# Loading the raw blocks of background jobs one unit ahead, in a mixture-of-experts kernel on one Trainium2 core

## The chip, the cores and the metric

The kernel runs on one core of a Trainium2 chip, as one launch. The metric is the device time of a launch in microseconds (us). Three runs of the kernel before took 2087.25, 2093.49 and 2100.9 us; the median, 2093.49, is the time to beat.

## The reference

Three layers follow each other on 2304 token rows of width 512: a windowed attention with global tokens, a mixture of 8 experts whose gate is normalised over rows and columns eight times, and a two-layer network with an ELU between.

```python
x = attention(q_l, k_l, v_l, q_g, k_g, v_g)         # (2304, 512) after the reshape
P = normalised_gate(x @ w_gate)                      # (2304, 8)
out = 0
for e in range(8):
    out += P[:, e:e+1] * (np.maximum(x @ w1[e], 0) @ w2[e])   # w1[e]: 512x1024, w2[e]: 1024x512
h = out @ w_in                                       # 512 x 2048
g = np.where(h > 0, h, np.exp(np.minimum(h, 0)) - 1)
return (g @ w_out).astype(np.float32)
```

## The kernel before, in words

**Arithmetic.** Every product of matrices is taken in two parts: an operand is split into a high part (suffix h) and a low rest (suffix l), and three matmuls (`three`, line 146: hh, lh, hl) replace one. Above that stands a scheme of Strassen's kind: a 2x2 block product is made of 7 block products, numbered 1 to 7, from sums and differences of blocks. Those sums have to be built, split and kept: x sums for the tokens, `t1`..`t4` for the weights.

**Units.** A unit is one half (512 of 1024 hidden columns) of one expert, so there are 16. The tokens are cut in two parts, and each unit is passed over twice.

- *First pass* (`mix_0`, line 1430), units 2 to 15, for the first 1024 rows: two chains of layer-one products (`01`..`07`, `11`..`17`) in the order of the string MIX_0, then layer two (`mix2`). A unit takes some 41 us. Work that isn't the unit's own is put into two lists and handed out between products: `side1` during layer one, `side2` (25 ticks) during layer two. They hold the loads, sums, splits and stores of the next unit's weights (`weights1`, `weights2`), which are also stored to DRAM for the second pass.
- *Second pass* (`mix_1`, line 1632), units 15, 2 to 14, 0, 1 (numbered a = 14 to 29), for the other 1280 rows in two halves, g = 0 (256 columns) and g = 1 (320). Chains `a` and `b` (class Fold) do layer one of the present half; `t` and `p` (class Tail, product n of it is `t1`, `p4`, ...) do layer two of the half before; `tx` is an extra piece of 64 rows. The string MIX_1 is the order of the products on TensorE (PE); a function hung on an event, such as `b3` or `t7`, is issued right behind that product. Prepared weights come back from DRAM (`load1`: wh, wl; `load2`: wfh, wfl).
- *Last layers*: the two-layer network, from the moment the last unit is done.

**Background jobs.** Beside its own work, each unit carries a job that prepares what is needed later. A *single* (`weights64`, SINGLES) and a *pair* (`weights64_pair`, units a = 22 to 29) turn blocks of w_out and w_in, which lie in memory as two 32-bit words a value, into high and low parts: a raw load (tensor r, line 1001), three operations of `words` and three of `sign` on VectorE (DVE), `value` or `parts` on ScalarE (ACT) and GpSimd (POOL), sums, splits, stores (wd of a single, wq of a pair, line 1080). `prepare` (PREPS) makes the weight sums of units 0 and 1 out of raw loads wr. BACK units fetch accumulated rows (yd, yr) and turn them (`x_pair`). In the second pass three raw buffers are shared by r, wr and yr.

**What sets the order.** Everything is written out by hand: engines carry out their instructions in the order of the program. All DMAs are issued by one engine, SyncE (SP), in that order; a transfer whose buffer isn't free or whose data isn't ready holds up all behind it. In the second pass before the change a unit's raw loads are issued as the unit begins, and its steps are handed out from there:

```python
lds, steps = jobs(a)
for f in lds:
    f()
```

**PSUM.** In the second pass 8 banks are dealt out by use: chains of product 1 have three (A), products 5 and 3 two (E), product 2 and `tx` two (m), the turning of x one (x).

Of the kernel before, what the change touches and what calls it, by code (L numbers as in the profile page):

```python
# [58 lines left out]
ROOM_1 = {**ROOM, "t": 2, "u2": 3, "u3": 1}  # L59
# [16 lines left out]
def tile_net(ctx: ExitStack, tc, kq, vw, vc, qg, wg, w1, w2, wi, wo, consts, out):  # L76
    nc = tc.nc
# [974 lines left out]
    def weights64_pair(u, k):  # L1052

        c0, c1 = Chunk(wi[u, :, k]), Chunk(wi[u, :, k + 2])

        def blk(n):
            return (c0, c1)[int(n[0]) - 1].t[:, 256 * (int(n[1]) - 1):256 * int(n[1])]

        def sums():
            t1, t3, t4, t2 = (c0.room(F32, 4)[:, i] for i in range(4))  # L1060
            for o, a, b in (
                (t1, blk("12"), blk("11")), (t3, blk("22"), blk("12")), (t2, blk("22"), t1), (t4, blk("21"), t2),
            ):
# [392 lines left out]
    fold = {"slots": {}, "v slots": deque(f"v{i}" for i in range(6)), "o slots": deque(f"o{i}" for i in range(14))}  # L1456
# [199 lines left out]
    with tc.manual_schedule():  # L1656
# [26 lines left out]
        def jobs(a):  # L1683
# [13 lines left out]
            return loads, steps  # L1697

# [11 lines left out]
        for a, u in enumerate(range(2, U1)):  # L1710
# [3 lines left out]
            side1.extend(loads1 + lds + [lambda u=u: store1(u)] + casts)  # L1714
            loads2 = []
# [32 lines left out]
        load2(units[0], ("11", "21", "t2", "t1", "t3", "t4", "22"))  # L1748
        tails = {}
        items = deque()  # L1750
        for n, u in enumerate(units):
# [3 lines left out]
            lds, steps = jobs(a)  # L1755
            for f in lds:
                f()
            for g in range(2):
                at = {}

                def add(e, f):
                    at.setdefault(e, []).append(f)

                if g == 0 and a in BACK:
                    j = BACK.index(a)
                    load_back(j)
                    xs_ = x_pair(2, j, lambda: (back[j][:, 0], back[j][:, 1]))
                    for e, f in zip("a6 b6 a5 b5 a7 b7 a4".split(), xs_):
                        add(e, f)
# [29 lines left out]
        at = {"t5": x0[:1], "t7": x0[1:3], "tx": x0[3:5], "t4": x0[5:6], "t3": x0[6:]}  # L1799
        at["t6"] = [lambda: load2(units[-1], ("12",))]  # L1800
# [161 lines left out]
```

## Time and profile before

| | |
|---|---|
| runs | 2087.25, 2093.49, 2100.9 us |
| profiled execution | 2103.94 us, of which the traced span is 2102.2 |
| PE | busy 1911.2 us, 91% of the span |
| DVE | 1491.6 us, 71% |
| ACT | 958.2 us, 46% |
| POOL | 407.4 us, 19% |
| granted PE clock, mean | 0.958 |

PE is the engine to look at: where it stands still, the end moves. A row of the timeline gives an instruction's start and duration and in brackets the idle time of its engine just before it, with what ended that idle time. The row of a windows table gives, for a stretch, the busy time of each engine, the mean granted clock of PE (1.00 is full, 2.4 GHz) and the mean share of the DMA engines.

### The profile page before, as it was taken

The numbers are of one execution on the slowest core, as the hardware profiler recorded it, in microseconds if no ns is written. First come the engines' busy times: TensorE is split into PE (matmuls) and PEld (weight loads), VectorE is DVE, ScalarE is ACT, GpSimd is POOL, SyncE is SP. The second block draws the span as 40 slices with busy tenths as digits, with TensorE's granted clock in tenths as the row PEclk, the third lists the DMA queues.
The fourth block names the chain that finished last, engine by engine and source line by source line (L and its number), as shares of the span: only waits on it lengthen the run. The fifth ranks groups of instructions, "written<-read, shape, count | busy, mean of one in ns | idle before, by whom it ended". The sixth has DMA issues, their size and how long they took to land.

```text
span 2102.2 us, 36329 instructions
## 1 busy us (share of the span) xinstructions
PE 1911.2 (91%) x13345; PEld 1690.2 (80%) x13345; DVE 1491.6 (71%) x2931; ACT 958.2 (46%) x2061; POOL 407.4 (19%) x390
## 2 busy tenths in 40 slices
PE   8999999999998986499999999888888869999999
PEld 6877778887887765489999999888888867788998
DVE  4555867777686663377777878777777758878887
ACT  5552443444433332254555544444444425545664
POOL 2135233223222221101010101111111100002322
PEclk9999999999999988799999999999999989999999
DMA  7686677687876758776867775555556686655431
GB/s 257 198 264 207 240 278 265 244 295 270 301 258 240 257 211 288 248 251 220 269 236 248 271 229 186 196 194 195 193 189 190 209 252 207 196 183 176 135 116 66
DMA packets 336754, 469.22 MB, mean 223 GB/s; under 512 B 32960, under 2 KB 210624, under 8 KB 332992
## 3 DMA queue, kind: packets, MB, share of 16 engines
q1 hardware_dynamic: 336576, 466.91, 65.9%
q8 instruction: 105, 1.72, 0.3%
q14 instruction: 73, 0.60, 0.1%
HBM read 282.12 MB, written 184.68 MB: 222 GB/s over the span
## 4 chain that ended last, share of the span: by engine, by line
PE 61%; DVE 14%; DMA 11%; SPq 6%; ACT 4%; issue 4%; POOL 1%; DVEq 0%; ACTq 0%; POOLq 0%
PE m L152 6%; PE m L148 6%; PE m L150 6%; PE f L1354 4%; PE f L1356 4%; PE f L1355 4%; PE f L1582 4%; PE f L1584 3%; PE f L1583 3%; PE q L1354 3%; SPq L1080 3%; DMA w2r<-in_w_dram 3%; PE q L1356 2%; PE q L1355 2%; DVE w2t L785 2%
## 5 line engine op out<-in xcount | busy, mean ns | idle before, releaser
L148 PE MATMUL m<-w2h,hh 128*128 128x512 f32 x784 | 309.9, 395 | 19.5 <-DVE acc L1426 13.8
L152 PE MATMUL m<-w2h,hl 128*128 128x512 f32 x784 | 310.3, 396 | 3.7 <-DVE hl L1264 3.4
L150 PE MATMUL m<-w2l,hh 128*128 128x512 f32 x784 | 309.5, 395 | 0.3 <-POOL w2l L144 0.2
L1028 POOL TENSOR_TENSOR cp<-r,cp 128x512 f32<-128x512 f32 x32 | 49.3, 1541 | 741.5 <-ACT r L1027 521.6
L148 PEld LDWEIGHTS m<-w2h,hh 128*128 128x128 f32 x784 | 148.2, 189 | 50.0 <-DVE acc L1426 14.3
L152 PEld LDWEIGHTS m<-w2h,hl 128*128 128x128 f32 x784 | 148.1, 189 | 38.5 <-DVE hl L1264 6.7
L150 PEld LDWEIGHTS m<-w2l,hh 128*128 128x128 f32 x784 | 148.4, 189 | 30.2 <-POOL w2l L144 1.4
L1498 ACT ACTIVATE v<-t 128x256 f32<-128x256 f32 (+1 forms) x192 | 83.4, 447 | 152.6 <-DVE t L785 152.5
L1582 PE MATMUL f<-wfh,hs 128*128 128x256 f32 x512 | 145.8, 285 | 4.5 <-ACT s L1590 4.5
L1584 PE MATMUL f<-wfh,ls 128*128 128x256 f32 x512 | 144.9, 283 | 0.0
L1583 PE MATMUL f<-wfl,hs 128*128 128x256 f32 x512 | 144.9, 283 | 0.0
L785 DVE TENSOR_TENSOR t<-f,u 128x256 f32<-128x256 f32 (+2 forms) x192 | 101.1, 531 | 56.9 <-ACT u L1360 34.4
L1264 POOL TENSOR_TENSOR hl<-eg,hh 128x288 fp32r<-128x288 f32 (+1 forms) x80 | 57.1, 722 | 354.5 <-DMA xs4h<-xo3h 224.0
L785 DVE TENSOR_TENSOR t<-q,u 128x512 f32<-128x512 f32 x56 | 38.7, 691 | 109.9 <-ACT u L1360 65.0
L144 POOL TENSOR_TENSOR w2l<-w2r,w2h 128x512 fp32r<-128x512 f32 x56 | 79.0, 1431 | 187.1 <-ACT w2h L140 187.1
L1582 PE MATMUL f<-wfh,h 128*128 128x256 f32 x384 | 109.7, 286 | 0.7 <-ACT u L1590 0.7
L1583 PE MATMUL f<-wfl,h 128*128 128x256 f32 x384 | 109.4, 285 | 0.0
L1584 PE MATMUL f<-wfh,l 128*128 128x256 f32 x384 | 109.4, 285 | 0.0
L1426 DVE SCALAR_TENSOR_TENSOR acc<-t,pr,acc 128x256 f32<-128x256 f32 x180 | 101.8, 606 | 3.2
L1354 PE MATMUL f<-xs1h,wh 128*128 128x256 f32 (+1 forms) x128 | 42.2, 329 | 67.9 <-DVE t L785 67.8
L1582 PEld LDWEIGHTS f<-wfh,hs 128*128 128x128 f32 x512 | 98.2, 192 | 5.6 <-ACT s L1590 5.5
L1583 PEld LDWEIGHTS f<-wfl,hs 128*128 128x128 f32 x512 | 98.2, 192 | 0.0
(402 smaller groups left out, 5927.2 us busy)
## 6 DMA issues: line engine op xcount, KB each, us to landing
wfh<-pw2h SPq DMA_DIRECT2D x128, 256.0 KB, 4.7
wfl<-pw2l SPq DMA_DIRECT2D x128, 256.0 KB, 5.2
wh<-pw1h SPq DMA_DIRECT2D x105, 256.0 KB, 5.1
wl<-pw1l SPq DMA_DIRECT2D x105, 256.0 KB, 5.2
pw1h<-wh SPq DMA_DIRECT2D x14, 1792.0 KB, 11.8
pw1l<-wl SPq DMA_DIRECT2D x14, 1792.0 KB, 15.2
wr<-in_w_dram SPq DMA_DIRECT2D x36, 512.0 KB, 7.3
w2r<-in_w_dram SPq DMA_DIRECT2D x28, 512.0 KB, 6.1
```

The costliest lines, as they stand in the source:

```text
L148: nc.tensor.matmul(ps, ah, bh, start=first, stop=False)
L150: nc.tensor.matmul(ps, ah, bl, start=False, stop=False)
L152: nc.tensor.matmul(ps, al, bh, start=False, stop=last)
L785: nc.vector.tensor_tensor(out=o, in0=a, in1=b, op=op)
L1354: nc.tensor.matmul(ps, wh, xh, start=k == 0 and i == b, stop=False, skip_group_check=True)
L1355: nc.tensor.matmul(ps, wh, xl, start=False, stop=False, skip_group_check=True)
L1356: nc.tensor.matmul(ps, wl, xh, start=False, stop=k == 1, skip_group_check=True)
L1426: nc.vector.scalar_tensor_tensor(out=acc, in0=y, scalar=scale, in1=acc, op0=ALU.mult, op1=ALU.add)
L1498: nc.scalar.activation(half[n, "v"][:, self.fp, :self.n], t, AF.Relu)
L1582: nc.tensor.matmul(ps[:, m], hh, wh, start=i == b and m == k == 0, stop=False, skip_group_check=True)
L1583: nc.tensor.matmul(ps[:, m], hh, wl, start=False, stop=False, skip_group_check=True)
L1584: nc.tensor.matmul(ps[:, m], hl, wh, start=False, stop=m == k == 1, skip_group_check=True)
```

## The change

The raw loads of a job move from the beginning of its unit into the unit before; at which slots of a unit a job's steps fall is now a table (SPOTS); jobs change units (SINGLES, BACK, PREPS); in the first pass the loads of w2 are issued in the middle of `side2` instead of at its end; at the second pass's beginning the yd stores stand behind three weight loads; at its end other orders are used and the operands of the last layers are loaded at other events; E has three PSUM banks, x none (the turning of x uses m), and `u3` two buffers.

```diff
-SINGLES = {0: 1, 1: 1, 2: 1, 4: 1, 6: 1, 8: 1, 10: 1, 11: 1, 12: 2, 13: 2, 15: 1, 17: 1, 19: 1, 21: 1}
-BACK = (15, 17, 19, 21)
-PREPS = {14: (0, 0), 16: (1, 0), 18: (0, 1), 20: (1, 1)}
+LAST_X = 12
+SINGLES = {0: 1, 1: 2, 2: 1, 4: 1, 6: 1, 8: 1, 11: 1, 12: 2, 16: 2, 18: 2, 20: 2}
+BACK = (14, 16, 18, 20)
+PREPS = {15: (0, 0), 17: (1, 0), 19: (0, 1), 21: (1, 1)}
 PAIRS = range(22, 30)
+SPOTS = {
+    "single": (6, 7, 9, 11, 12, 13, 15, 17),
+    "pair": ((9, 11, 12, 14, 16, 17, 20), (2, 4, 6, 7, 8, 9)),
...
-MIX_1 = "a1 b1 p4 a2 b2 p3 a6 b6 a5 b5 a7 b7 t1 a4 b4 t6 a3 b3 t2 t5 t7 tx"
+MIX_1 = "a1 b1 p4 a2 b2 p3 a6 b6 a5 b5 a7 b7 t1 a4 b4 a3 t6 b3 t2 t5 t7 tx"
-MIX_E = "p4 p3 t1 t2 t6 t5 t7 tx t4 t3"
+MIX_E = "p4 p3 t1 t2 t6 t5 t7 t4 t3 tx"
-ROOM_1 = {**ROOM, "t": 2, "u2": 3, "u3": 1}
+ROOM_1 = {**ROOM, "t": 2, "u2": 3}
...
-                ps = [bank(m).tile([128, 4, 128], F32, tag=m, name="x2t") for m in "mx"]
+                ps = [bank(m).tile([128, 4, 128], F32, tag=m, name="x2t") for m in "mm"]
...
-        m, n = {1: ("A", 3), 5: ("E", 2), 2: ("m", 2)}[i]
+        m, n = {1: ("A", 3), 5: ("E", 3), 2: ("m", 2)}[i]
...
-                steps = steps + [ld] + ws
+                loads, steps = loads + [ld], steps + ws
...
+        def item(a, before, ats, lists):
+            loads, steps = jobs(a)
+            if a in BACK:
+                j, g = BACK.index(a), int(a == BACK[0])
+                (ats[0] if g else before[1]).setdefault("b3", []).append(lambda: load_back(j))
+                for e, f in zip("a6 b6 a5 b5 a7 b7 a4".split(), x_pair(2, j, lambda: (back[j][:, 0], back[j][:, 1]))):
+                    ats[g].setdefault(e, []).append(f)
+                at, places = ats[0], (None, SPOTS["single"])
+            else:
+                at, places = before[1], SPOTS["last" if a == LAST else "pair" if a in PAIRS else "prepare"]
+            for e, f in zip(("b3", "t7"), loads):
+                at.setdefault(e, []).append(f)
...
             if build1:
-                side2.extend(mingle(mingle(build1, build2), steps))
+                side2.extend(mingle(build2, build1[:8]))
+                loads2, casts, build2 = weights2(u + 1)
+                side2.extend(loads2 + mingle(build1[8:], steps))
...
-            if u + 1 < U1:
-                loads2, casts, build2 = weights2(u + 1)
-                side2.extend(loads2)
             mix_0(u, at)
-        for i in range(TP[0] // 128):
-            nc.sync.dma_start(yd[:, i], accs[i])
...
-        load2(units[0], ("11", "21", "t2", "t1", "t3", "t4", "22"))
+        load2(units[0], ("11", "21", "t2"))
+        for i in range(TP[0] // 128):
+            nc.sync.dma_start(yd[:, i], accs[i])
+        load2(units[0], ("t1", "t3", "t4", "22"))
...
-            lds, steps = jobs(a)
-            for f in lds:
-                f()
+            if nxt is not None:
+                item(a + 1, ats, *plan)
...
-                            add(e, lambda x=x, names=names: (operands(2, (x,), 256, SL), layer_one(0, 0, names), layer_one(0, 1, names)))
+                            add(e, lambda x=x: operands(2, (x,), 256, SL))
+                        for e, w in zip("t1 t2 t6 t5 t7".split(), W22):
+                            add(e, lambda w=w: layer_one(0, 0, (w,)))
...
-        at = {"t5": x0[:1], "t7": x0[1:3], "tx": x0[3:5], "t4": x0[5:6], "t3": x0[6:]}
-        at["t6"] = [lambda: load2(units[-1], ("12",))]
+        at = {"p4": [lambda: layer_one(0, 0, W22[5:6])], "p3": [lambda: layer_one(0, 0, W22[6:])]}
+        at["t6"] = [lambda: load2(units[-1], ("12",)), *x0[:2]]
+        at.update({"t5": x0[2:3], "t7": [*x0[3:5], lambda: layer_one(0, 1, W22[:4])]})
+        at.update({"t4": [*x0[5:6], lambda: layer_one(0, 1, W22[4:])], "t3": x0[6:]})
```

Three places of the order, before and now.

SP in a pair unit of the second pass, before: the six rows of a pair's stores (r, cp, ct into wqh and wql), and what is issued next.

```order
L899 DMA wl<-pw1l 128x512
L1080 DMA wqh<-r_13984 128x2x128 x3
L1080 DMA wqh<-cp 128x2x128 x3
L1080 DMA wqh<-r_13984 128x2x128
L1080 DMA wql<-r_13982 128x2x128 x3
L1080 DMA wql<-ct 128x2x128 x3
L1080 DMA wql<-r_13982 128x2x128
L1001 DMA r_14620<-in_wi_dram 128x1024
L1001 DMA r_14622<-in_wi_dram 128x1024
L1630 DMA wfh<-pw2h 128x512
```

The same loads now:

```order
L907 DMA wl<-pw1l 128x512
L1009 DMA r_14572<-in_wi_dram 128x1024
L1009 DMA r_14627<-in_wi_dram 128x1024
L1640 DMA wfh<-pw2h 128x512
L1640 DMA wfl<-pw2l 128x512
```

The next pair's raw loads were the row behind the stores, and ran as its unit began; now eight weight loads lie between the stores and them, and they are issued within g = 1 of the unit before their steps.

SP where the second pass begins, before: the last stores of prepared w2 (pw2l), the yd stores, seven wf weights, the raw loads wr of the first job.

```order
L1001 DMA r_8311<-in_wo_dram 128x1024
...
L932 DMA pw2l<-w2l 128x2x256 x4
L1728 DMA yd<-acc_111 128x512
...
L1728 DMA yd<-acc_118 128x512
L1630 DMA wfh<-pw2h 128x512
L1630 DMA wfl<-pw2l 128x512
...
L967 DMA wr<-in_w_dram 128x1024 x2
```

Now:

```order
L940 DMA pw2l<-w2l 128x2x256 x4
L1640 DMA wfh<-pw2h 128x512
L1640 DMA wfl<-pw2l 128x512
...
L1780 DMA yd<-acc_111 128x512
...
L1780 DMA yd<-acc_118 128x512
...
L1691 DMA yr<-yd 128x512 x2
```

Three wf pairs stand ahead of the yd stores, no raw load of a single is left near them, and the first unit's job is now the fetch of yr, with wr a unit later.

ACT at the boundary behind a first-pass unit with two singles (a = 12), before: r is a single's block, wh and w2ht are splits of the next unit's weights, s the copy of a product that the next unit's products wait for.

```order
L1027 ACTIVATE r_7846<-r_7846 128x512
L1041 CAST r_7846<-ct 128x512
...
L919 CAST w2ht_7959<-w2t_7910 128x512
L865 CAST wh<-wt_7964 128x512
L1027 ACTIVATE r_7936<-r_7936 128x512
L1041 CAST r_7936<-ct 128x512
L919 CAST w2ht_7989<-w2t_7949 128x512
L865 CAST wh<-wr 128x512
L1360 COPY s_8037<-q_8030 128x512
```

Now:

```order
L873 CAST wh<-wt_7889 128x512
L1035 ACTIVATE r_7709<-r_7709 128x512
L1049 CAST r_7709<-ct 128x512
L873 CAST wh<-wt_8001 128x512
L1035 ACTIVATE r_7718<-r_7718 128x512
L1049 CAST r_7718<-ct 128x512
L873 CAST wh<-wr 128x512
L1370 COPY s_8051<-q_8044 128x512
```

Both singles now lie directly ahead of s; the splits of w2 have gone ahead of both.

## Rows read from the trace of the kernel before

**Rows 1.** Windows table: PE, PEld, DVE, ACT, POOL busy (x instructions), clock, DMA share, GB/s.
```profile
core 0 of [0], span 2102.2 us
200.00:830.00 630.00, 595.74 (x2555) 484.49 (x2554) 433.44 (x676) 245.03 (x436) 175.61 (x122) 0.97 0.74 266
830.00:893.00 63.00, 25.51 (x144) 24.07 (x144) 25.52 (x45) 13.52 (x30) 8.34 (x6) 0.68 0.65 228
893.00:1250.00 357.00, 338.73 (x2520) 330.60 (x2519) 269.12 (x520) 187.63 (x428) 23.10 (x16) 0.98 0.74 247
1250.00:1690.00 440.00, 380.03 (x2794) 374.17 (x2793) 338.94 (x613) 200.08 (x462) 78.09 (x64) 0.93 0.61 198
1690.00:1740.00 50.00, 33.70 (x211) 30.18 (x210) 26.66 (x51) 13.94 (x27) 0.00 (x0) 0.83 0.80 239
1740.00:2102.00 362.00, 351.37 (x1811) 300.23 (x1809) 293.83 (x526) 198.77 (x434) 57.08 (x80) 1.00 0.49 152
```

**Rows 2.** Waits, 1250 to 1690: us in total, times, longest.
```profile
PE f L1354 <- DVE t L785: 59.9, 8, 8.8
DVE ct L1008 <- DMA r<-in_wi_dram: 43.9, 8, 6.8
```

**Rows 3.** Timeline of PE, DVE and SP (its DMA issues) around one boundary of pairs.
```profile
1378.87 0.58 PE L1354 MATMUL f<-xs1h,wh 128*128 128x256 f32 x1 [7.62 <-DVE t L785]
...
1372.49 0.43 DVE L1008 TENSOR_SCALAR ct<-r 128x512 int32<-128x512 int32 x1 [5.62 <-DMA r<-in_wi_dram]
1373.75 0.87 DVE L1426 SCALAR_TENSOR_TENSOR acc<-f,pr,acc 128x256 f32<-128x256 f32 x2
...
1378.85 2.90 DVE L1426 SCALAR_TENSOR_TENSOR acc<-t,pr,acc 128x256 f32<-128x256 f32 x2
...
1367.61 1.00 SPq L1001 DMA_DIRECT2D r<-in_wi_dram  x2
```

**Rows 4.** Windows: behind a gap, a whole pair unit, a unit without one, a first-pass stretch.
```profile
1375.40:1382.20 6.80, 3.33 (x15) 3.33 (x16) 6.70 (x11) 3.59 (x10) 2.64 (x2) 0.50 0.01 2
...
1600.37:1655.22 54.85, 47.19 (x349) 46.49 (x349) 42.09 (x77) 24.78 (x57) 9.81 (x9) 0.94 0.62 197
...
943.00:993.00 50.00, 47.47 (x350) 46.76 (x351) 40.87 (x78) 25.78 (x59) 6.71 (x5) 0.97 0.63 214
...
310.00:675.00 365.00, 361.94 (x1579) 295.58 (x1578) 261.61 (x389) 147.49 (x262) 105.71 (x74) 1.00 0.75 273
```

**Rows 5.** Timeline where the second pass begins: PE, DVE, POOL, SP.
```profile
838.66 0.80 PE L148 MATMUL m<-w2h,hh 128*128 128x512 f32 x1 [13.85 <-DVE acc L1426]
855.75 0.58 PE L1354 MATMUL f<-x12h,wh 128*128 128x256 f32 x1 [9.94 <-DVE acc L1426]
881.07 0.58 PE L1354 MATMUL f<-xs3h,wh 128*128 128x256 f32 x1 [18.89 <-ACT u L1360]
...
833.21 0.43 DVE L1008 TENSOR_SCALAR ct<-r 128x512 int32<-128x512 int32 x1 [19.36 <-DMA r<-in_wo_dram]
...
878.83 1.26 POOL L974 TENSOR_TENSOR wt<-wr 128x512 f32<-128x512 f32 x1 [25.97 <-DMA wr<-in_w_dram]
...
827.33 0.45 SPq L1001 DMA_DIRECT2D r<-in_wo_dram  x1
857.69 5.86 SPq L1728 DMA_DIRECT2D yd<-acc  x8
```

**Rows 6.** Timeline of PE where the second pass ends.
```profile
1722.27 0.76 PE L148 MATMUL f<-wfh,heh 128*128 128x512 f32 x1 [15.62 <-DMA wfh<-pw2h]
```

**Rows 7.** Waits in the first pass, 190 to 830.
```profile
ACT w2h L140 <- DMA w2r<-in_w_dram: 46.0, 13, 7.8
...
PE q L1354 <- ACT s L1360: 24.9, 9, 8.1
```

**Rows 8.** Timeline of ACT and PE at the boundary behind a first-pass unit.
```profile
676.68 0.62 ACT L1041 CAST r<-ct 128x512 fp32r<-128x512 f32 x1 [6.78 <-POOL cp L1028]
...
679.40 0.80 PE L1354 MATMUL q<-xs2h,wh 128*128 128x512 f32 x1 [6.26 <-ACT s L1360]
```

More of the change, by code (lines that the diff above doesn't have):

```diff
@@ L44 @@
 AHEAD = (3, 5, 7, 9)
-SINGLES = {0: 1, 1: 1, 2: 1, 4: 1, 6: 1, 8: 1, 10: 1, 11: 1, 12: 2, 13: 2, 15: 1, 17: 1, 19: 1, 21: 1}
-BACK = (15, 17, 19, 21)
-PREPS = {14: (0, 0), 16: (1, 0), 18: (0, 1), 20: (1, 1)}
+LAST_X = 12
+SINGLES = {0: 1, 1: 2, 2: 1, 4: 1, 6: 1, 8: 1, 11: 1, 12: 2, 16: 2, 18: 2, 20: 2}
+BACK = (14, 16, 18, 20)
+PREPS = {15: (0, 0), 17: (1, 0), 19: (0, 1), 21: (1, 1)}
 PAIRS = range(22, 30)
+LAST = PAIRS[-1]
+SPOTS = {
+    "single": (6, 7, 9, 11, 12, 13, 15, 17),
+    "pair": ((9, 11, 12, 14, 16, 17, 20), (2, 4, 6, 7, 8, 9)),
+    "last": ((6, 7, 8, 9, 10, 11, 14, 16, 17, 18, 19, 20, 21), None),
+    "prepare": (range(7, 22), range(6)),
+}
 XT = NT - 1
@@ L1071, in hi, with lo @@
             nc.scalar.copy(c1.room(F32R, 4), c0.room(F32, 4))
-        def lo():
-            for t, h in ((c1.t, c1.p), (blk("11"), c0.p[:, :256]), (c0.room(F32, 4), c1.room(F32, 4))):
-                comb(t.bitcast(F32R), t, h, ALU.subtract)
+        def lo(i):
+            t, h = ((c1.t, c1.p), (blk("11"), c0.p[:, :256]), (c0.room(F32, 4), c1.room(F32, 4)))[i]
+            comb(t.bitcast(F32R), t, h, ALU.subtract)
         def store():
@@ L1080, in store @@
                     nc.sync.dma_start(wq[q][:, u, i, :, k], v.rearrange("p (f c) -> p f c", f=2))
-        return [c0.load, c1.load], [c0.words, c0.sign, c0.value, c1.words, c1.sign, c1.value, sums, plain, hi, lo, store]
+        return [c0.load, c1.load], [
+            c0.words, c0.sign, c0.value, c1.words, c1.sign, c1.value, sums, plain, hi, *(lambda i=i: lo(i) for i in range(3)), store
+        ]
     def x_pair(p, j, rows):
@@ L1454, in mix_0 @@
         pop(side2, len(side2))
-    fold = {"slots": {}, "v slots": deque(f"v{i}" for i in range(6)), "o slots": deque(f"o{i}" for i in range(14))}
+    fold = {"slots": {}, "v slots": deque(f"v{i}" for i in range(5)), "o slots": deque(f"o{i}" for i in range(14))}
     def slot(kind, *of):
@@ L1695, in jobs @@
                 ld, ws = weights64(*singles.popleft())
-                steps = steps + [ld] + ws
+                loads, steps = loads + [ld], steps + ws
             return loads, steps
+        def item(a, before, ats, lists):
[10 more added lines that the diff above has]
+                at.setdefault(e, []).append(f)
+            steps = deque(steps)
+            for g in range(2):
+                if places[g] and steps:
+                    lists[g].extend([None] * 22)
+                    for i in places[g]:
+                        if steps:
+                            lists[g][i] = steps.popleft()
+            assert not steps
         def mingle(long, short):
@@ L1713, in tile_net @@
             loads1, build1 = weights1(u + 1) if u + 1 < U1 else ([], [])
-            side1.extend(loads1 + lds + [lambda u=u: store1(u)] + casts)
-            loads2 = []
+            side1.extend(loads1 + lds + ([lambda u=u: store1(u)] if build1 else []) + casts)
+            if a == LAST_X:
+                side1.append(lambda: second_x(XUSE, SL, HALF))
             if u + 1 == U1:
@@ L1719, in tile_net @@
             if build1:
-                side2.extend(mingle(mingle(build1, build2), steps))
-            else:
-                side2.extend([lambda: second_x(XUSE, *GS[1])] + mingle(build2, steps))
-            if u + 1 < U1:
-                loads2, casts, build2 = weights2(u + 1)
-                side2.extend(loads2)
+                side2.extend(mingle(build2, build1[:8]))
+                loads2, casts, build2 = weights2(u + 1)
+                side2.extend(loads2 + mingle(build1[8:], steps))
+            else:
+                side2.extend([lambda: second_x(XUSE, GS[1][0], SL)] + mingle(build2, steps))
             mix_0(u, at)
-        for i in range(TP[0] // 128):
-            nc.sync.dma_start(yd[:, i], accs[i])
         pools["stack"].close()
@@ L1747, in tile_net @@
         units = (U1 - 1, *range(2, U1 - 1), 0, 1)
[L1748 removed]
+        load2(units[0], ("11", "21", "t2"))
+        for i in range(TP[0] // 128):
+            nc.sync.dma_start(yd[:, i], accs[i])
+        load2(units[0], ("t1", "t3", "t4", "22"))
         tails = {}
         items = deque()
+        plan = ([{}, {}], [[], []])
+        item(14, None, *plan)
         for n, u in enumerate(units):
@@ L1754, in tile_net @@
             before = units[n - 1] if n else None
-            lds, steps = jobs(a)
-            for f in lds:
-                f()
+            (ats, lists), plan = plan, ([{}, {}], [[], []])
+            if nxt is not None:
+                item(a + 1, ats, *plan)
             for g in range(2):
-                at = {}
+                at = ats[g]
                 def add(e, f):
[L1762 to L1769, printed above, removed]
+                    at.setdefault(e, []).insert(0, f)
                 if g == 0 and n:
@@ L1784, in tile_net @@
                     else:
-                        for e, x, names in zip(
-                            "b1 b2 b6 b5 b7 b4 b3".split(), XUSE, ((),) * 4 + (("11", "t2", "21", "t3", "t1"), ("t4",), ("22",))
-                        ):
-                            add(e, lambda x=x, names=names: (operands(2, (x,), 256, SL), layer_one(0, 0, names), layer_one(0, 1, names)))
+                        for e, x in zip("b1 b2 b6 b5 b7 b4 b3".split(), XUSE):
+                            add(e, lambda x=x: operands(2, (x,), 256, SL))
+                        for e, w in zip("t1 t2 t6 t5 t7".split(), W22):
+                            add(e, lambda w=w: layer_one(0, 0, (w,)))
                 state = {"done": []}
-                half = len(steps) if g else 0 if a in BACK else len(steps) // 2
-                items.extend(steps[:half])
-                steps = steps[half:]
+                items.extend(lists[g])
                 order = (MIX_1 if nxt is not None or g == 0 else MIX_L).split()
```

## The prediction

> **What bounds the kernel now.** I read four views. First the table of stretches [rows 1]: PE is the busiest engine in each, and what it lacks of a stretch is what can be won. It lacks little from 1740 on, which the change hardly touches, and most in four places: where the second pass begins (25.51 busy of 63), in the pair units 1250 to 1690 (380.03 of 440), where the second pass ends (33.70 of 50) and, thinly, in the first pass. Then the waits, the timeline and the windows of single units, for what ended PE's idle time and what that waited for in turn.
>
> - *Pair units.* PE waits eight times for a DVE copy, 59.9 us in all; DVE waits eight times for the raw load r, 43.9 us, 5.5 each [rows 2]. At one boundary [rows 3]: SP issues r at 1367.61, DVE has stood still for 5.62 us when it begins `words` at 1372.49, and PE stands still for 7.62 us up to 1378.87, since the copy it needs is queued on DVE behind `words` and what piled up. Behind such a gap the clock is 0.50, and 3.33 us of PE work were done at it [rows 4]: 1.67 us lost on top.
> - *Beginning.* Three gaps, 13.85, 9.94 and 18.89 [rows 5]. The first two end with an `acc` on DVE, which had stood 19.36 us for a single's raw load issued at 827.33, in the first pass's last unit. In the third, the raw loads wr of the first `prepare` stand on SP behind the yd stores (5.86 us) and fourteen weight loads; POOL waits 25.97 us for them, and ACT's copies wait for POOL.
> - *End.* One gap, 15.62, on a wfh load [rows 6]: block "12", which stands on SP behind the loads of the last layers' operands.
> - *First pass.* PE waits 24.9 us in nine places for ACT's s copy [rows 7]. ACT is late by waits for w2r loads (46.0 us, 13 times) [rows 7], or because a single's cast, waiting 6.78 us for POOL, stands ahead of s: PE then waits 6.26 [rows 8].
>
> **The most that can be won**, by place, at 1.67 us of slow clock [rows 4] for each long gap:
> 1. First pass: 630 - 595.74 = 34.3 idle [rows 1]; the first gap of [rows 5] began at 824.8, so 5.2 of it belong to the beginning: 29.1. Ten such waits would lose 16.7 of clock; most are short, I take 10. Together 39.
> 2. Beginning: 13.85 + 9.94 + 18.89 = 42.7, and 3 x 1.67 = 5.0: 47.7.
> 3. Units a = 14 to 21: 357 - 338.73 = 18.3, and at a mean clock of 0.98 [rows 1] up to 7.1: 25.4.
> 4. Pairs: 59.9 + 8 x 1.67 = 73.3.
> 5. End: 15.62 + 1.67 = 17.3.
>
> In all 202.7 us of the profiled execution's 2103.94 (span 2102.2 [rows 1]), which is 10.45, or 0.5%, above the median of the runs. I take what is won here from the median.
>
> **The change, part by part.**
>
> *Pairs.* Nothing is added: the same loads, steps and stores, `lo` in three pieces. The loads are issued in g = 1 of the unit before, tens of us before `words`, so DVE's 5.5 goes. What is late next is DVE itself: 42.09 us busy of a unit's 54.85 [rows 4]. PE's own work is 47.19 - 1.67 = 45.5 a unit, so DVE would be busy 92% of it and in g = 0, where seven of the thirteen steps lie, some us behind. Lower bound of the gain: only the load's wait goes, 8 x 5.5 = 44. Upper: 73. The nearest row is 943 to 993: DVE busy 40.87 of 50 without a raw wait of a pair, PE idle 2.53 [rows 4]. A third E bank lets PE go on by one product while DVE is behind, and `t6` now comes behind `a3`, so I take 1.4 lost a unit, somewhat over half of that row: 73 - 8 x 1.4 = **62**.
>
> *Beginning.* The last first-pass unit has no single now, so DVE's 19.36 has no cause; unit 14 fetches yr and makes no weight sums, so POOL's 25.97 has none. The yd stores, still 5.86 us of SP, stand behind the three wf pairs needed first; four pairs follow them. Bounds: 0 and 47.7. What is late next is the round trip of the last w2 sums through DRAM to wf, or yr behind yd. PE comes to wf only after layer one of unit 14, so I leave 6 for it: **42**.
>
> *End.* "12" is still issued at `t6`, but layer one's loads are spread over five products and `tx` stands last, so that less is ahead of it. Bounds 0 and 17.3; I take **16**.
>
> *First pass.* The w2 loads in the middle of `side2` come half a layer two earlier, tens of products ahead of the casts that waited 46.0, so I take that away. But the steps of singles now lie in the second half of `side2`, just ahead of the next unit's s on ACT (the third piece of the order). From 310 to 675, singles in the middle cost nearly nothing: PE 361.94 of 365 at clock 1.00 [rows 4]. A single at the boundary cost 6.26 and 1.67 of clock, 8 us [rows 8]. So ten singles cost between 0 and 80, against 39 that are won. I take 2 us where a unit has one (6 units) and 8 where it has two (2 units, the second single having nothing behind it to hide in): 28. Net **10**; bounds +39 and -41.
>
> *Units 14 to 21.* Six singles (four before), two in each BACK unit but the first; `prepare` and singles have their raw data a unit early. The turning of x takes both m banks, so product 2 can wait for it: between 0 and 2.5 us for each of four turns, the idle time of a unit that has one now [rows 4]. I take a bit less than half of the 25.4: **12**. E's third bank and `u3`'s second buffer cost no instruction.
>
> Sum: 62 + 42 + 16 + 10 + 12 = 142 us. From 2103.94 that is 1962; from the median, 2093.5 - 142 = **1951.5**, which I predict.
>
> **The rivals.**
>
> *B. DVE is the bound of the pair units.* For: 92% busy is much for an engine that also waits for PE and ACT. If its other idle time stays, 54.85 - 42.09 - 5.5 = 7.3, a unit takes 49.4 and the pairs give 44: 1969.5. It can be more, by the sums on POOL: the `acc` pair that ran beside one took 2.90 us, another 0.87 [rows 3], and POOL is busy 9.81 us a unit [rows 4]. If all of that held DVE, which loses about 2 to it now, DVE would need 42.1 + 7.8 = 49.9, the pairs give 40, and the time is 1974. The Trainium skill, "SBUF — State Buffer", section "Who interferes with whom", says that a DVE instruction with two SBUF inputs contends with a GpSimd instruction that reads SBUF, and that the later one is blocked in full; the 2.90 against 0.87 agrees with that. Against: the steps are now spread over slots, so that DVE has other work's gaps between them. Chance 0.16.
>
> *C. The boundary of first-pass units.* Each single costs the 8 us of [rows 8]: 80 lost against 39 won, the pass is 41 slower: 1951.5 + 10 + 41 = 2002.5. For: every single now lies there. Against: its raw load is on time, and ACT has only two copies for each. Chance 0.10.
>
> *D. The loads don't come earlier.* At b3 and t7 a raw load waits on SP for one of three raw buffers, whose last reader is the store of the job before. Then r lands as late as now, and pairs and units 14 to 21 give nothing: 2093.5 - 42 - 16 - 10 = 2025.5. Against: the load at 1367.61 stood directly behind the stores, and both issues took 1.00 us in all [rows 3], so even there a buffer was free; now eight loads lie between. Chance 0.06; together with C, 2077, within 1%, 0.02.
>
> *E. Slower: SP held by the raw loads.* The same wait, but longer, and what stands behind it decides: wf and wh loads of the present unit follow r on SP, so PE would wait for weights at all 15 boundaries of the second pass. It has to eat 142 us to be no gain, 9.5 a unit; with the 21 us that make it measurably slower, 10.9. At 12 us it is 1951.5 + 180 = 2131. Against: the same row as against D. Chance 0.04.
>
> **How the numbers follow.** The forecast has 0.62, and its own range is 1918 to 1985: at the fast end the first pass gives 25 and the pairs and units 14 to 21 ten more together, at the slow end the first pass loses 10 and the beginning keeps ten. B lies inside, C at the upper edge. Without D, D with C, and E (0.12), and with 0.05 below, the range is 1912 to 2004. About 1%, 21 us, is what can be told from no change. Faster by more: forecast, B, C and D, 0.94. Within it: D with C, 0.02. Slower: E, 0.04.
>
> **What would show it.** In the profile after: no `DVE ct <- DMA r<-in_wi_dram` in the pair units, and units 46 to 47.5 us apart (B: 49 or more, PE still waiting for DVE's t; D: the DMA wait stays). No gap over 6 us between 825 and 890 of the old time. The "12" load landed before `t3` needs it. In the first pass, waits of PE for ACT's s, about 2 us behind units with one single and 8 behind those with two, none for w2r. The prediction is wrong in its mechanism if the pair units stay above 50 us without a raw wait, if the first pass takes longer than before, or if SP shows weight loads held behind r.

## The result, and the profile after

The changed kernel took 2028.51 us (median of 4 runs, 2023.33 to 2028.89) against 2096.33 before on the same chip: a ratio of 0.9676, 95% interval 0.9638 to 0.9714. It is faster by 68 us, where 142 were forecast, and it lies above the range (1912 to 2004). The two profiled executions lie 75 us apart (2103.94 and 2028.89), since the one before took 7.6 us more than its median; the places below add up to 77, and ahead of the first pass 2 us are lost.

To compare places, both traces are cut at the same matmuls: the first of layer one of the first pass, then the first of units a = 14, 15, 22 and 29 of the second pass, its last layer-one matmul, and the end. Windows of the kernel before (length, then busy time of PE, PEld, DVE, ACT, POOL, clock, DMA share, GB/s):

```profile
207.60:843.50 635.90, 592.98 (x2533) 482.09 (x2532) 435.83 (x673) 244.72 (x435) 173.10 (x120) 0.96 0.73 263
843.50:906.80 63.30, 33.77 (x230) 32.84 (x229) 25.95 (x47) 21.18 (x49) 6.72 (x5) 0.78 0.77 265
906.80:1255.80 349.00, 331.42 (x2469) 323.78 (x2469) 263.33 (x510) 180.72 (x411) 23.10 (x16) 0.98 0.72 243
1255.80:1639.50 383.70, 331.48 (x2439) 326.58 (x2438) 295.49 (x535) 173.64 (x399) 68.62 (x56) 0.93 0.60 194
1639.50:1687.20 47.70, 39.95 (x289) 38.99 (x288) 37.79 (x69) 21.91 (x51) 9.47 (x8) 0.93 0.68 219
1687.20:2098.30 411.10, 387.87 (x2043) 333.21 (x2041) 321.29 (x579) 214.15 (x463) 57.08 (x80) 0.98 0.53 164
```

The same six places of the changed kernel:

```profile
209.60:822.70 613.10, 585.70 (x2534) 478.11 (x2533) 431.55 (x664) 247.39 (x432) 167.12 (x119) 0.98 0.75 263
822.70:869.90 47.20, 34.19 (x238) 33.70 (x237) 21.70 (x41) 19.26 (x45) 0.00 (x0) 0.86 0.89 298
869.90:1220.30 350.40, 332.33 (x2461) 321.29 (x2461) 272.09 (x527) 181.27 (x418) 32.34 (x22) 0.99 0.75 256
1220.30:1578.60 358.30, 330.96 (x2439) 323.82 (x2438) 302.09 (x532) 173.98 (x399) 67.98 (x56) 0.97 0.64 208
1578.60:1623.20 44.60, 39.61 (x289) 38.85 (x288) 39.70 (x69) 22.26 (x51) 10.25 (x8) 0.96 0.61 200
1623.20:2023.40 400.20, 388.29 (x2043) 333.24 (x2041) 321.29 (x578) 213.16 (x463) 56.75 (x80) 0.99 0.55 170
```

Subtract the lengths: first pass -22.8 (13.85 of it the gap that I counted to the beginning), unit 14 -16.1, units 15 to 21 +1.4, units 22 to 28 -25.4, unit 29 -3.1, rest -10.9. The largest miss is the pair units. They take 51.2 us each, 54.8 before, where 47 were forecast, and DVE is busy *longer* than before in them, 302.09 instead of 295.49, with 532 instructions against 535.

The waits of the changed kernel from 1220 to 1578 (us, times, longest) no longer have DVE waiting for r; PE's wait has another releaser than in [rows 2], the scaled addition `acc`:

```profile
PE f L1364 <- DVE acc L1436: 22.4, 7, 3.2
```

The timeline of the changed kernel ahead of one such wait: PE, then the DVE rows that tell, then POOL.

```profile
1405.12 0.41 PE L1364 MATMUL f<-x12h,wh 128*128 128x320 f32 x1 [3.20 <-DVE acc L1436]
...
1387.50 1.75 DVE L793 TENSOR_TENSOR l<-v,h 128x512 fp32r<-128x512 f32 x1
1389.17 1.78 DVE L793 TENSOR_TENSOR ls<-os,hs 128x512 fp32r<-128x512 f32 x1
...
1395.18 1.80 DVE L793 TENSOR_TENSOR v<-v,v 128x512 f32<-128x512 f32 x1
1396.90 0.41 DVE L793 TENSOR_TENSOR t<-f,u 128x256 f32<-128x256 f32 x1
1397.24 1.45 DVE L793 TENSOR_TENSOR l<-v,h 128x512 fp32r<-128x512 f32 x1
...
1399.32 1.81 DVE L1436 SCALAR_TENSOR_TENSOR acc<-t,pr,acc 128x256 f32<-128x256 f32 x2
1401.06 1.22 DVE L793 TENSOR_TENSOR os<-v,os 128x512 f32<-128x512 f32 x1
...
1403.71 0.68 DVE L793 TENSOR_TENSOR l<-v,h 128x512 fp32r<-128x512 f32 x1
1404.32 0.74 DVE L1436 SCALAR_TENSOR_TENSOR acc<-f,pr,acc 128x512 f32<-128x512 f32 x1
...
1387.38 1.32 POOL L1036 TENSOR_TENSOR cp<-r,cp 128x512 f32<-128x512 f32 x1 [36.84 <-DVE cp L1026]
1388.77 1.62 POOL L1040 TENSOR_TENSOR ct<-ct,cp 128x512 f32<-128x512 f32 x1
1394.80 1.63 POOL L1036 TENSOR_TENSOR cp<-r,cp 128x512 f32<-128x512 f32 x1 [4.40 <-DMA wfh<-pw2h]
1396.51 1.62 POOL L1040 TENSOR_TENSOR ct<-ct,cp 128x512 f32<-128x512 f32 x1
1398.10 1.87 POOL L1072 TENSOR_TENSOR r<-ct 128x256 f32<-128x256 f32 x2
1399.93 1.80 POOL L1072 TENSOR_TENSOR r<-ct,r 128x256 f32<-128x256 f32 x2
```

PE had ended `tx` by 1397; the `acc` that empties its bank is run at 1404.32, since DVE is that far behind. None of the DVE rows has a bracket: between 1375 and 1409 the trace shows no wait of it. But l takes 1.75 and 1.45 us while a POOL sum runs, and 0.68 when none does, at 1403.71. From 1374.7 to 1411 DVE is busy 35.15 of 36.3 us, and six of its rows (those of 1.22 to 1.81 us above) are 5.5 us longer together than the same instructions alone.

```profile
1363.00:1374.70 11.70, 11.70 (x94) 11.70 (x93) 4.84 (x10) 5.22 (x12) 0.00 (x0) 1.00 0.94 286
1374.70:1411.00 36.30, 32.40 (x237) 31.38 (x236) 35.15 (x62) 18.78 (x44) 9.72 (x8) 0.95 0.55 185
```

Just ahead, in g = 1, lie 11.7 us in which DVE is busy 4.84 and POOL not at all: all eight POOL sums of the unit fall into the full stretch.

The change did not bring this about. In the kernel before, the stretch behind the wait for r holds all eight sums too, at the unit of [rows 3]:

```profile
1372.49:1411.00 38.51, 32.13 (x228) 31.64 (x229) 35.45 (x63) 19.18 (x44) 9.80 (x8) 0.91 0.51 178
```

Beside POOL's sums DVE's instructions are longer than alone by 4.3 us a unit there (30.1 in units 22 to 28, each instruction against the median of its own kind with no POOL instruction beside it), and by 5.5 now (38.4). So some 4.3 of the 42.09 us that DVE was busy in a unit [rows 4] were such lengthening.

### The profile page after: what moved, and what is told of

It reads as the page before. It is cut to its first block, busy times and chain, and to the rows that moved or that the text cites. A ratio compares the mean times of both kernels' runs of the same rounds, so it can differ in the third digit from the quotient of the medians.

```text
span 2027.1 us, 36412 instructions
## 1 busy us (share of the span) xinstructions
PE 1905.1 (94%) x13345; PEld 1682.2 (83%) x13345; DVE 1500.2 (74%) x2931; ACT 958.9 (47%) x2061; POOL 403.1 (20%) x390
## 4 chain that ended last, share of the span: by engine, by line
PE 34%; DVE 15%; DMA 5%; issue 2%; ACT 1%; SPq 1%; POOL 1%; DVEq 0%; POOLq 0%; ACTq 0%
PE f L1364 3%; PE f L1366 3%; PE f L1365 3%; PE m L160 3%; PE m L156 3%; PE m L158 3%; PE f L1592 3%; PE f L1594 3%; PE f L1593 3%; DVE t L793 2%; PE q L1312 2%; PE q L1311 2%; PE q L1310 2%; DVE acc L1436 2%; DVE ls L793 2%
## 5 line engine op out<-in xcount | busy, mean ns | idle before, releaser
L1592 PEld LDWEIGHTS f<-wfh,hs 128*128 128x128 f32 x512 | 102.3, 200 | 3.9 <-ACT s L1600 3.6
L1594 PEld LDWEIGHTS f<-wfh,ls 128*128 128x128 f32 x512 | 101.5, 198 | 0.0
L1399 ACT ACTIVATE hh<-t 128x512 fp32r<-128x512 f32 x84 | 53.2, 633 | 81.2 <-DVE t L793 81.1
```

Of the source, the lines that this page charges most:

```text
L1592: nc.tensor.matmul(ps[:, m], hh, wh, start=i == b and m == k == 0, stop=False, skip_group_check=True)
L1594: nc.tensor.matmul(ps[:, m], hl, wh, start=False, stop=m == k == 1, skip_group_check=True)
```

## The experiments

All are edits of the changed kernel. Times are medians of runs, each beside the kernel before on the same chip (2096.8 to 2097.5 there); the interval is that of the ratio to it, to be held against 0.9676, whose own interval is 0.9638 to 0.9714.

### Why the pair units take 51 us

**1. POOL's sums of a pair left out.**

```diff
...
-c0.words, c0.sign, c0.value, c1.words, c1.sign, c1.value, sums, plain,
+c0.words, c0.sign, c0.cast_only, c1.words, c1.sign, c1.cast_only, lambda: None, plain,
```

> The changed kernel with a pair's three kinds of sums on GpSimd (POOL) left out (the mult and add of each chunk and the four block differences), so that the prepared w_in holds no usable values; DVE, ACT, loads and stores stay. Theory 1, contention: in the changed kernel's pair unit DVE works 36 us without a pause, and six of its instructions take 5.5 us longer while POOL's sums run (1.75, 1.78, 1.80, 1.45, 1.81, 1.22 us instead of 0.69, 0.68, 0.68, 0.69, 0.88, 0.68). Without POOL they are short again, PE's waits of 3.2 and 0.7 us a unit and the 1.7 of slow clock behind them go, units fall from 51.2 to about 46.5: 2028 - 8 x 4.7 = 1990. Theory 2, place of the steps: DVE is full there because the steps' own work (some 8 us a unit) lies in g=0; then POOL matters little, at most 1.5 us a unit: 2016 or more. Theory 3, banks: PE waits for one of two m banks whatever DVE does: 2028.

1986.79 us, ratio 0.946 (0.9421 to 0.9499): theory 1. Units 22 to 28:

```profile
1216.00:1532.90 316.90, 316.90 (x2439) 313.45 (x2438) 262.85 (x532) 174.83 (x399) 0.00 (x0) 1.00 0.70 233
```

PE is never idle, at 45.3 us a unit, with the steps' slots, the loads and the banks as they were. DVE does the same 532 instructions in 262.85 instead of 302.09 us: POOL's sums cost it 5.6 us a unit.

**2. All steps of a pair in g = 1.**

```diff
-    "pair": ((9, 11, 12, 14, 16, 17, 20), (2, 4, 6, 7, 8, 9)),
+    "pair": ((), (5, 6, 7, 8, 9, 10, 11, 12, 13, 14, 15, 16, 18)),
```

> The changed kernel with all thirteen steps of a pair in slots 5 to 18 of g=1, none in g=0 (the last unit stays). DVE stands still there for some 7 us of a unit now. Theories 1 and 2: the steps and POOL's sums move to where DVE has idle time, DVE is on time where g=1 begins, the wait of 3.2 for the eviction of tx goes; a unit takes 46 to 48: 1990 to 2004. Theory 3, banks: the wait stays, 2028. A rival on the other side: the stores, issued at slot 18, and the raw loads behind them hold up wf loads on SP, and PE waits for wf by some us a unit: 2035 or more.

2031.51 us, 0.9677 (0.9636 to 0.9718): no gain, which theory 1 had not foreseen. The wait for `acc` is gone, but PE has two others. Ahead of the first, for DVE's t, two operations of `words` that take 0.43 us alone last 1.42 and 1.40 beside a POOL sum. Ahead of the second, for ACT's s, ACT stands still at `plain`, which follows too close on POOL's sums. DVE stands still at `lo` for the same reason, behind the first wait:

```profile
1354.90 1.42 DVE L1017 TENSOR_SCALAR ct<-ct 128x512 f32<-128x512 f32 x1
...
1364.96 1.03 DVE L793 TENSOR_TENSOR ct<-ct,cp 128x512 fp32r<-128x512 f32 x2 [4.88 <-POOL r L1072]
...
1362.10 0.62 ACT L1075 CAST cp<-ct 128x512 fp32r<-128x512 f32 x1 [1.92 <-POOL ct L1040]
...
1359.73 0.42 PE L1364 MATMUL f<-xs4h,wh 128*128 128x320 f32 x1 [1.38 <-DVE t L793]
1363.56 0.39 PE L1592 MATMUL f<-wfh,hs 128*128 128x256 f32 x1 [2.69 <-ACT s L1600]
```

**3. Two E banks and one x bank, as before.**

```diff
-        m, n = {1: ("A", 3), 5: ("E", 3), 2: ("m", 2)}[i]
+        m, n = {1: ("A", 3), 5: ("E", 2), 2: ("m", 2)}[i]
...
-                ps = [bank(m).tile([128, 4, 128], F32, tag=m, name="x2t") for m in "mm"]
+                ps = [bank(m).tile([128, 4, 128], F32, tag=m, name="x2t") for m in "mx"]
```

> The changed kernel with two E banks and one x bank as before the change. If the third E bank is what carries PE over DVE's lag in g=0, PE waits there again by about 3 us a pair unit and loses clock: 2050 to 2065. If the raw load was all, 2028 plus or minus 5. Theory 1 and 2: some 1 to 2 us a unit in 16 units, 2035 to 2055.

2033.62 us, 0.969 (0.9644 to 0.9736). Whether the third bank is worth 5 us or none can't be told; it isn't what carries the change. The pair units take 51.2 us here too (358.5 in seven).

**4. A pair's raw loads in their own unit.**

```diff
+            if a in PAIRS:
+                for e, f in zip(("a1", "b1"), loads):
+                    ats[0].setdefault(e, []).append(f)
+                loads = []
```

> The changed kernel with a pair's two raw loads issued behind a1 and b1 of their own g=0, as before the change about, with the steps at the changed slots (the first behind the tenth product). If it is the later slots that took away DVE's wait for the raw load, nothing changes: 2028 plus or minus 6, no DMA wait on DVE. If the load one unit ahead did it, DVE waits again some 3 to 5 us a unit: 2050 to 2065.

2028.24 us, 0.9661 (0.9623 to 0.9698): the same, and DVE waits for no raw load. At one boundary the two loads are issued at 1371.82 and `words` begins at 1381.80, 10 us later; in [rows 3] DVE stood ready for `words` when the loads were issued. In the changed kernel it is the later slots, the first behind the tenth product, that end the wait of [rows 3]; the load a unit ahead adds nothing to them. Whether that load would have ended the wait with the steps at their old slots was not run.

**5. POOL's part in slots 4 to 6 of g = 1.**

```diff
-c0.words, c0.sign, c0.value, c1.words, c1.sign, c1.value, sums, plain,
+c0.words, c0.sign, c1.words, c1.sign, c0.value, c1.value, sums, plain,
...
-    "pair": ((9, 11, 12, 14, 16, 17, 20), (2, 4, 6, 7, 8, 9)),
+    "pair": ((9, 12, 14, 17), (4, 5, 6, 8, 10, 11, 12, 13, 15)),
```

> The changed kernel, nothing left out: of a pair, words and sign of both chunks stay in g=0 (slots 9, 12, 14, 17), all that POOL does is put into g=1 (slots 4 to 6), where DVE has some 7 us to spare, then plain, hi and the three parts of lo (to slot 13) and the store (slot 15). Theory 1, contention at the full stretch of DVE: the unit comes near that without POOL (45.3): 46 to 47.5, so 1990 to 2003. If instead DVE waits for POOL's sums in g=1 by 4 to 5 us, as where all steps lay there, the waits of 1.4 and 2.7 stay: 2025 to 2032.

2023.16 us, 0.9655 (0.962 to 0.9691): both of the expected cases missed. ACT, which carries out its instructions in order too, now waits for POOL ahead of the copies u that PE needs:

```profile
1351.34 0.62 ACT L1075 CAST cp<-ct 128x512 fp32r<-128x512 f32 x1 [3.37 <-POOL ct L1040]
1354.66 1.04 ACT L1079 CAST r<-r 128x1024 fp32r<-128x1024 f32 x1 [2.39 <-POOL r L1072]
...
1356.08 0.41 PE L1364 MATMUL f<-x22h,wh 128*128 128x320 f32 x1 [3.61 <-ACT u L1370]
```

**6. The same, with ACT's and DVE's steps behind POOL put off.**

```diff
-    "pair": ((9, 12, 14, 17), (4, 5, 6, 8, 10, 11, 12, 13, 15)),
+    "pair": ((9, 12, 14, 17), (4, 5, 6, 11, 13, 14, 15, 16, 18)),
```

> As the run with POOL's part of a pair in slots 4 to 6 of g=1, but ACT's two copies behind it (plain, hi) wait until slots 11 and 13, lo until 14 to 16, the store until 18. There PE waited 3.61 us a unit for ACT's u, which stood behind plain (3.37 us of waiting for POOL) and hi (2.39). If that wait in ACT's row was all that was left, units fall to 46 to 47.5: 1990 to 2003. If the lengthened DVE instructions (1.65, 2.24, 1.78 us) or the late lo keep PE waiting somewhere else, 2010 to 2026.

1988.02 us, 0.9467 (0.9448 to 0.9486). Nothing is left out, and units 22 to 28 have no idle time of PE:

```profile
1226.80:1543.60 316.80, 316.80 (x2438) 313.36 (x2437) 286.22 (x532) 174.67 (x399) 63.18 (x56) 1.00 0.71 232
```

DVE's instructions are lengthened here too, by 23.4 us in the seven units (286.22 against 262.85 without sums), but in g = 1, where it has time. Ahead of and beside POOL's sums in this kernel:

```profile
1301.32 1.65 DVE L793 TENSOR_TENSOR l<-v,h 128x512 fp32r<-128x512 f32 x1
1302.90 0.68 DVE L793 TENSOR_TENSOR t<-f,u 128x512 f32<-128x512 f32 x1
1303.62 2.25 DVE L1436 SCALAR_TENSOR_TENSOR acc<-t,pr,acc 128x256 f32<-128x256 f32 x2
...
1302.51 1.63 POOL L1040 TENSOR_TENSOR ct<-ct,cp 128x512 f32<-128x512 f32 x1
```

t, one of whose inputs f is a PSUM bank, isn't lengthened in the midst of a POOL sum (0.68); l, both of whose inputs lie in SBUF, is.

**7. A pair's sums done by DVE, in the changed kernel's slots** (the mult and the add of each chunk alike).

```diff
...
-                nc.gpsimd.tensor_tensor(out=o, in0=a, in1=b, op=ALU.subtract)
+                comb(o, a, b, ALU.subtract)
...
```

> The changed kernel with a pair's sums done by DVE instead of POOL, in the same slots; nothing else. DVE gets eight instructions more, 4 x 0.69 + 4 x 0.41 = 4.4 us a unit, in the stretch where it has no pause. Theory 1, contention: the 5.5 us by which POOL lengthens DVE's instructions go, so DVE is relieved in spite of the added work: 50 us a unit, 2015 to 2025, not slower than the changed kernel. Rival, the amount of DVE work (POOL's sums cost DVE nothing, and leaving them out helped by ending waits for their results): 4.4 us are added to a full stretch, 55 us a unit, 2045 to 2065.

2013.28 us, 0.9596 (0.958 to 0.9612). This tells contention from the amount of work: DVE does 56 instructions more and is nevertheless busy less, 290.57 against 302.09, and the kernel is faster. The amount counts as well: a unit takes 48.7 us, and PE still waits up to 2.4 us for `acc`.

```profile
1221.50:1562.40 340.90, 323.46 (x2439) 316.33 (x2438) 290.57 (x588) 172.60 (x399) 0.00 (x0) 0.99 0.67 218
```

Against the kernel without sums, DVE's own sums cost it 27.7 us in seven units, POOL's 39.2.

**8. The sums by DVE, in slots 6 to 8 of g = 1** (the order of steps that of 5).

```diff
-    "pair": ((9, 11, 12, 14, 16, 17, 20), (2, 4, 6, 7, 8, 9)),
+    "pair": ((9, 12, 14, 17), (6, 7, 8, 9, 10, 11, 12, 13, 15)),
...
```

> Words and sign of a pair stay in g=0 (slots 9, 12, 14, 17); the sums are done by DVE in slots 6 to 8 of g=1, where it has some 7 us to spare, then plain, hi and lo to slot 13, the store at 15. Theory 1: nothing is lengthened, no engine waits for POOL, units fall to 45.5 to 47 us: 1986 to 2000. If DVE is full whatever is done (rival: the amount), 2020 or more.

1999.27 us, 0.9531 (0.9515 to 0.9546); 47.1 us a unit. PE waits 1.6 us a unit for an ACT copy.

### The other places

**9. The yd stores and yr ahead of wf.**

```diff
...
-        load2(units[0], ("11", "21", "t2"))
         for i in range(TP[0] // 128):
             nc.sync.dma_start(yd[:, i], accs[i])
+        load_back(0)
+        load2(units[0], ("11", "21", "t2"))
         load2(units[0], ("t1", "t3", "t4", "22"))
```

> The changed kernel with the yd stores and, behind them, the load of yr issued ahead of all seven wf pairs where the second pass begins. There PE waits 10.0 us for yr, whose load stands on SP behind three wf pairs, the eight yd stores (5.70 us) and four wf pairs. Theory, the queue: yr is issued some 9 us earlier, the wait and the slow clock behind it go, and wf still lands ahead of layer two: 10 to 13 us faster than the changed kernel, 2016 to 2018. Rival, the round trip: yr can't land earlier, since the stores must land first; the wait stays above 7 us: 2026. Rival on the other side: wf is late, and PE waits for it instead: 2028 or more.

2018.01 us, 0.9614 (0.9582 to 0.9647), which overlaps a little with the changed kernel's interval. In the changed kernel, PE and SP at the beginning of the second pass:

```profile
852.06 1.94 PE L1107 MATMUL x2t<-ident,yr 128*128 128x128 f32 x8 [10.00 <-DMA yr<-yd]
...
835.78 5.70 SPq L1780 DMA_DIRECT2D yd<-acc  x8
846.61 0.96 SPq L1691 DMA_DIRECT2D yr<-yd  x2
```

With yr first that wait falls to 0.3: the queue, not the round trip. Unit 14 takes 36.0 instead of 47.2 us. Part of that is lost again in this kernel: units 15 to 21 take 358.4 instead of 350.5 us. PE now comes to the first `prepare` before its raw load wr is there, and waits 3.44 us for an ACT copy that stands behind 5.60 us of waiting for POOL.

**10. Steps of singles in the first half of side2.**

```diff
-                side2.extend(mingle(build2, build1[:8]))
+                side2.extend(mingle(mingle(build2, build1[:8]), steps))
                 loads2, casts, build2 = weights2(u + 1)
-                side2.extend(loads2 + mingle(build1[8:], steps))
+                side2.extend(loads2 + build1[8:])
```

> The changed kernel with the steps of singles in the first half of side2, ahead of the w2 loads, instead of the second. PE now waits for ACT's s at eight unit boundaries: 1.7 us behind a unit with one single (six times, 2.0 and 1.7), 7.2 and 7.9 behind those with two; 27.4 idle and 7.0 of slow clock in the pass. Theory, the place of the steps: the waits go, 25 to 33 us faster: 1996 to 2004. Rival, the amount: ACT and POOL need the same time in all and the next unit's splits are late instead; less than 10 us: 2019 or more.

2018.66 us, 0.9627 (0.9605 to 0.9649). Of the 27.4 us of waiting for s in the first pass 21.4 are left, and 1.3 for a DVE copy are new: the changed kernel's 1.69 become 1.30, its 7.94 become 6.84, and the pass is 6.9 us shorter. Mostly the amount, then, not the place: with the singles ahead, the next unit's own splits are late. A sum of theirs on POOL holds ACT up right ahead of s.

```profile
438.00 0.50 PE L1364 MATMUL q<-xs2h,wh 128*128 128x512 f32 x1 [1.69 <-ACT s L1370]
781.39 0.80 PE L1364 MATMUL q<-xs2h,wh 128*128 128x512 f32 x1 [7.94 <-ACT s L1370]
```

Those two rows are the changed kernel's. In the run with the singles early, ahead of the wait of 6.84:

```profile
772.13 0.62 ACT L873 CAST wh<-wt 128x512 fp32r<-128x512 f32 x1 [4.84 <-POOL wt L869]
```

### The parts together

Three of these, with the last steps of `prepare` at every third slot of g = 1 (`range(0, 18, 3)` for `range(6)`), since ACT waited 6.52 us for a store to free a buffer there:

```profile
1001.88 0.62 ACT L986 CAST wh<-wr 128x512 fp32r<-128x512 f32 x1 [6.52 <-DMA pw2h<-wh]
...
1004.49 0.42 PE L1364 MATMUL f<-xs3h,wh 128*128 128x320 f32 x1 [3.35 <-ACT u L1370]
```

**11. With experiment 5 (edits 5, 9, 10).**

> The three edits together (yr first, singles early, POOL later), and the last six steps of the prepare job spread over every third slot of g=1, so that ACT doesn't wait (6.5 us at two units) for a store to leave one of its two buffers. If each gain stands by itself: 2028 - 12 - 28 - 30 - 8 = 1950; what the parts measure, added, plus or minus 6.

1997.18 us, 0.9523 (0.9497 to 0.9549), within 6 us of what the parts measured, added (5 gave little). The wait of 3.35 is gone. The spread `prepare` was not run alone.

**12. With experiment 8 (edits 8, 9, 10).**

> That edit of the pairs, with yr first, singles early and the prepare job spread, all in one. The run with those three and POOL's sums in g=1 took 1997. If the pairs gain by themselves what theory 1 says (some 30 to 38 us against that run), 1958 to 1968.

1975.21 us, 0.9415 (0.9383 to 0.9447), above the expected 1958 to 1968. The pair units take 47.1 us as in 8; the miss was not taken apart.

**13. With experiment 6 (edits 6, 9, 10).**

> The version of the pairs without any idle time of PE (POOL's part in slots 4 to 6 of g=1, ACT's copies and lo late), with yr first, singles early and the prepare job spread. The place table of the runs gives 2028 - 41 (pairs) - 11 (a = 14) - 7 (first pass) - 5 (a = 15 to 21): 1958 to 1970 if the parts add up. If the spread prepare job or the early singles put work back in front of the pairs, 1975 or more.

1961.57 us, 0.9349 (0.9327 to 0.9372): they add up.

**14. And one single moved.**

```diff
-SINGLES = {0: 1, 1: 2, 2: 1, 4: 1, 6: 1, 8: 1, 11: 1, 12: 2, 16: 2, 18: 2, 20: 2}
+SINGLES = {0: 1, 1: 2, 2: 1, 4: 1, 6: 1, 8: 1, 11: 1, 12: 1, 13: 1, 16: 2, 18: 2, 20: 2}
```

> The same with the second single of unit a = 12 moved to unit a = 13, which has none. Behind units with two singles PE still waits 6.84 us for ACT's s although the steps were put into the first half of side2; behind units with one 1.3. If the amount of work in the unit sets that wait, it falls to about 1.3 behind a = 12, with 1.7 of slow clock, and where the second pass begins PE waits 1 to 3 us longer for DVE: 4 to 7 us faster. If the place alone sets it, 6.84 stays. If DVE then waits for the raw load again in the first pass's last unit (as before the change, 19.4 us), 10 us or more slower.

1953.13 us, 0.9313 (0.9289 to 0.9338), the fastest of all: 8 us faster than 13, a little more than expected, and the first pass is 9.3 us shorter. The wait behind unit 12, in the kernel of 13 and in this one:

```profile
770.25 0.80 PE L1364 MATMUL q<-xs2h,wh 128*128 128x512 f32 x1 [6.84 <-ACT s L1370]
```

```profile
762.88 0.50 PE L1364 MATMUL q<-xs2h,wh 128*128 128x512 f32 x1 [1.30 <-ACT s L1370]
```

So the amount sets that wait; at unit 1, which still has two singles, 6.83 stays.

## Why the prediction was wrong, point by point

- **Pairs, -62: the step that failed; measured -25.4 in units 22 to 28 and -3.1 in unit 29.** It is the residual, "1.4 lost a unit": 51.2 - 45.3 = 5.9 were lost. PE's idle time is (358.30 - 330.96) / 7 = 3.9 of it, and the slow clock behind the waits (330.96 - 316.90) / 7 = 2.0. The sign put down for a wrong mechanism came: units above 50 us without a raw wait. I had summed DVE's work over the unit, 92%, and taken it as fitting. But the time is decided by a stretch of 36 us in which DVE is full, and by when POOL runs in it. Experiments 1, 6 and 7 show that POOL's sums, in that stretch, are the cause. They had lain there before the change too, behind the raw load's wait, and DVE's 42.09 held some 4.3 us of lengthening by them, of which I had counted about 2, and that in rival B alone. The reasons for halving the loss of the nearest row, a third bank and `t6` behind `a3`, had no number. Experiment 3 takes the bank away, and the units stay at 51.2; the place of `t6` was not tried.
- **Rival B** had named the mechanism, at 49.4 to 49.9 us a unit. That this is near 51.2 is in part luck: it counted up to 49.9 us of DVE work, and DVE is busy 302.09 / 7 = 43.2. It too took DVE over the whole unit, and left out the slow clock behind each wait. The rule of the Trainium skill, "SBUF — State Buffer", section "Who interferes with whom", is that a DVE instruction with two SBUF inputs contends with a POOL instruction that reads SBUF, and that one with at most one SBUF input, outside the modes in which it uses two ports, does not. Experiment 6 agrees: beside a POOL sum l, with both inputs in SBUF, took 1.65 us instead of 0.68, and t, with one input in PSUM, 0.68.
- **The load a unit ahead.** The wait for r did go, as forecast, but experiment 4 shows that the later slots did it. Rivals D and E are refuted too: no raw load waited for a buffer, and PE waits for no load in units 22 to 28, and 1.2 us at most in units 15 to 21.
- **Beginning, -42.** Both old causes went, and with them the gaps of 13.85 and 18.89. But a gap over 6 us is left, which the prediction had ruled out: "yr behind yd", to which I left 6, took 10.0 and slow clock (experiment 9), and 3.0 for an `acc` stayed. Together with the first pass, from its start to unit 15, 39 of 52 came.
- **First pass, net -10.** Its waits came out about as sized, and ACT's waits for w2r are gone: 3.5 behind the first unit with one single, 1.7 to 2.0 behind the other five, 7.2 and 7.9 behind the two with two. The reason was half right: the amount of steps more than their place (experiments 10 and 14). Rival C is refuted.
- **Units 15 to 21, -12: measured +1.4.** I took half of the cap with no mechanism behind it. The denser `prepare` made ACT wait for a store (6.52), and short waits stayed; with its last steps spread, in the combined runs, that wait is gone.
- **End, -16: measured -10.9.** The gap of 15.62 is gone; waits of PE for other weight loads, 1.9, 0.9 and 0.7 us, are left. In unit 29, where all thirteen steps lie in g = 0, PE waits 4.99 us for DVE; two operations of `words` ahead of that take 1.53 and 1.37 us instead of 0.43 beside POOL's sums. No run took this apart.

The sum was out by 33 in the pairs, 13 each in the beginning with the first pass and in units 15 to 21, and some 5 at the end, 65 in all. The rest of the 77 us is mostly the 10.45 us by which the profiled execution, in which the places were measured, lay above the median that the sum was taken from. The range failed because it held the residual of the pairs to what one engine's average load allows.

## What to carry to other kernels

When a wait is removed, look at the stretch behind it for the engine that will then be full, not at its share of the whole unit; and look at what another engine will run beside it there. Compare one and the same instruction along the stretch: an engine that never waits can still lose time in instructions that are lengthened. Work given to POOL isn't free to DVE: put it where DVE has idle time, and put everything in an in-order queue that needs its result well behind it. If there is no such place, DVE may do the work in less of its own time than POOL costs it.

## What the runs showed of the hardware

A DVE operation of 128x512 with two SBUF inputs that began while a POOL sum ran took 1.22 to 1.80 us instead of 0.68 in the rows of the changed kernel; with one input in PSUM it took 0.68 as alone (experiment 6). Operations with one tensor input were lengthened too: in experiment 2 two of `words` took 1.42 and 1.40 us instead of 0.43. The eight sums of a pair cost DVE 39.2 / 7 = 5.6 us a unit when POOL did them in DVE's full stretch, 23.4 / 7 = 3.3 when POOL did them in g = 1, and 27.7 / 7 = 4.0 when DVE did them itself.
